# Gated infini-attention and SwiGLU on one core: six operands of x taken over from the first stage, eight made beside its last chains, fills of the stacks apart, and the feature map ahead of the remainder

## The chip, the cores and the metric

The kernel runs on one core of a Trainium2 chip. The metric is the device time of one execution in microseconds (us); the time before is the median of three runs. The engines are named as the profile names them: PE is the matrix engine, with PEld its weight loads, DVE the vector engine, ACT the scalar engine, POOL the engine called GpSimd, and SP the engine that issues the DMAs; SPq is its queue.

## The reference

The input `x` has 2048 rows of D = 576. A gate for each row mixes a memory-augmented attention with a feed-forward network.

```python
g = sigmoid((x * gate_w).sum(-1))              # one number per row
# a: H = 32 heads of 18, S = 2048 in 4 segments of L = 512
phi = where(t > 0, t + 1, exp(t))
for s in range(4):
    p = softmax(qs @ ks.T * 18 ** -0.5 + causal_mask)
    a_mem = (phi(qs) @ M) / (phi(qs) @ z + 1e-6)
    o = sigmoid(beta) * a_mem + (1 - sigmoid(beta)) * (p @ vs)
    M, z = M + phi(ks).T @ vs, z + phi(ks).sum()
a = concat(o) @ wo
# b: F = 4608
b = (silu(x @ w_gate) * (x @ w_up)) @ w_down
out = g * a + (1 - g) * b
```

## The kernel before

The products of the projections, of the network and of `wo` keep fp32 accuracy by splitting: `split(hi, lo, src)` (L103 to L105) writes a rounded copy of an operand on ACT (the high half) and the remainder on DVE (the low half), and PE multiplies high by high, high by low and low by high. A *chain* is one bank of PSUM filled by 14 such matmuls (`products`, L127). PSUM has eight banks; a small cycle of banks belongs to each kind of work, so a product waits until its bank has been read out.

**First stage (0 to about 231 us).** It works through the four segments of 512 rows.

- Nine `qk` chains of a segment make `q` and `k` transposed. Each result is split three ways into bf16 parts in `q3`: a copy on ACT (L314), the remainder `qr` on DVE (L315), its copy on ACT (L324), the last part on POOL (L325). SP stores `q3` to DRAM (`stk`), two chains later (`late`, `flush`). Chains whose feature map is wanted also make `ph`: Relu (L322) and Exp (L323) on ACT, then a combination on DVE (L327). In the list `mid` a caller may put work of its own between `qr` and Relu.
- Eight `v_step`s make `v` in banks 5, 6 and 7. Each has a plain copy `vf` (ACT, in segment 0 DVE, L345), a first bf16 part `vps` (ACT, L346), the remainder `r1` (DVE, L347), the second part (ACT) and the third (POOL), and in its second half a copy of the gate's logit, `gl` (DVE, L349). Beside them the next segment's x is split, one tile in a step.
- `upd_gen` updates the memory matrix during the next segment's chains: transposes, a copy `kt` on ACT (L378), the accumulating matmuls L369, then the masks (L389 to L393). `mem_step` reads the memory beside the `v_step`s (L415 to L422), and its result `om` goes to DRAM (`med`).

The x operands live in seven slots of two tiles, `xo00` to `xo61`, each with a high and a low half of 128 x 512. A segment's x fills slots 0 and 1 (segments 0 and 2) or 5 and 6 (segments 1 and 3); slots 2, 3 and 4 are staging for loads.

**Second stage.** The gate and up projections of the network use a scheme of seven block products (`seven`, L917) instead of eight: the operands of x are the blocks `c, d, e, g` of two segments and sums of them (`XO[0]` to `XO[6]`, two tiles `z` each; the sums are made in place on POOL by `x_sum`), and the weights likewise. One pass (`half`) covers segments 2 and 3, a second one segments 0 and 1. Each pass goes over 36 tiles `f` of 128 columns of F. A loop written out by hand runs the seven products of a tile, reads out the banks in between, and calls `tick` eight times; a tick runs `beat`, which first runs what `defer(k, fn)` has queued for that beat in `due`, then a share of the down projection (`down_group`, L765 and L770) and a step of the attention's generator (`att_gen`: scores L602 and L642, exp L646, the mask L654, casts L719 and L721, products with v L671 and L673). In the first pass `w_make(f)` makes the weight operands of the next tile: sums on POOL (`total`, L231), high halves on ACT (L235), low halves on DVE (L238), and SP keeps them in DRAM (`wc`, L248), from where the second pass fetches them.

**Between the stages.** After the last chains of segment 3, the memory of the q weights (pool `qp`) is closed and pools for the weights open in its place. `x_first()` loads eight x tiles of 256 KB into a pool `xrp` of its own, and returns a list of 14 steps: a split for each of the seven operands and two `z`, eight of them followed by a sum on POOL (L154 to L160). Two such steps are run in each of the `v_step`s 2 to 7 as far as four are left. The first weight operands (`start = w_make(0)`) begin in `v_step` 3, with up to 0, 3, 3, 6, 6 steps from there on; the rest of both lists is run ahead of the second stage. Then four stack tiles `kst` are filled with -1 by POOL (L587), the buffers `mb` with 0, and `stack_load(0)` issues the stack loads from `stk` on SP (L188), all in program order.

**Ahead of the end.** When the attention's generator is exhausted, `c_open` queues ten `wo_load`s. With n from 1 to 10, a load of 128 x 288 goes into one of three `woraw` buffers at beat n, the cast on ACT (L800) comes at beat n + 2, the low half on DVE (L801) at n + 3. The final loop then multiplies the attention by `wo`, mixes and stores.

Of the kernel before, what the change touches and what calls it, by code (L numbers as in the profile page):

```python
# [12 lines left out]
F32 = mybir.dt.float32  # L13
# [19 lines left out]
NT = 5  # L33
# [13 lines left out]
BREAK = 10  # L47
KR = 6 * DH
# [7 lines left out]
def gated_mix(ctx, tc, xT, wf, wd, wv, wo, beta, cmask, ident, bmask, out):  # L56
# [211 lines left out]
    with ExitStack() as st:  # L268
# [20 lines left out]
        def q_split(m, u):  # L289
            split(qw[m][0][:, u], qw[m][1][:, u], raws[m, u])  # L290
# [17 lines left out]
        def qk(s, m, u, mid=()):  # L308
            t = chain_tile()
            hi, lo = qw[m]  # L310
            products(t, w_stat(hi[:, u], lo[:, u]), x_side(*xs_of[s]))
# [3 lines left out]
            nc.vector.tensor_sub(qr, t, q3[:, 0])  # L315
            for fn in mid:
                fn()
            ph = None
            if m == 4 or (u == 0 and s > 0) or (u == 1 and s < 3):
                ph = sp.tile([P, L], F32, name=f"ph{m}{u}", bufs=2 if m == 4 else 1)  # L320
                phi[s, m, u] = ph
                nc.scalar.activation(ph, t, AF.Relu, scale=-1.0)  # L322
                nc.scalar.activation(ph, ph, AF.Exp, scale=-1.0)  # L323
            nc.scalar.activation(q3[:, 1], qr, AF.Copy)  # L324
            nc.gpsimd.tensor_sub(q3[:, 2], qr, q3[:, 1])  # L325
            if ph is not None:
                nc.vector.scalar_tensor_tensor(ph, t, 0.0, ph, op0=OP.max, op1=OP.add)  # L327
            if m < 4:
                late.append((stk[u, s, m * P:m * P + P], q3))
            else:  # L330
                for kind in range(2):
                    late.append((stk[kind, s, 512:D], q3[64 * kind:64 * kind + 64]))

        def v_step(s, hf, i):
# [7 lines left out]
            if s:  # L342
                nc.scalar.activation(fv, pv, AF.Copy)
            else:
                nc.vector.tensor_copy(fv, pv)  # L345
            nc.scalar.activation(v[:, i, :, 0, 0:DH], pv, AF.Copy)  # L346
            nc.vector.tensor_sub(r1, pv, v[:, i, :, 0, 0:DH])  # L347
            if hf:
                nc.vector.tensor_copy(gl[:, 4 * s + i:4 * s + i + 1], t[:, 288:289])  # L349
# [124 lines left out]
        def x_first():  # L474
            r = [[xrp.tile([P, L], F32, name=f"xr{b}{kt}") for kt in range(4)] for b in range(2)]
            for z in range(2):
                for b, kt in ((0, z), (1, z), (1, 2 + z), (0, 2 + z)):
                    nc.sync.dma_start(r[b][kt], xT[HALF[0][b], :, kt])
            X = [[None, None] for _ in range(7)]

            def four(z):
                return r[0][z], r[1][z], r[0][2 + z], r[1][2 + z]

            def one(j, z):
                c, d, e, g = four(z)
                X[j][z] = x_slot(j, z)
                split(X[j][z][:, 0], X[j][z][:, 1], (c, c, c, e, d, g, e)[j])
                for i, back in ((0, 1), (1, 2), (2, 4), (3, 6)):
                    if j == i:
                        x_sum(back, *four(z))  # L490

            return X, [lambda j=j, z=z: one(j, z) for j in range(7) for z in range(2)]

        for s in range(NSEG):
            upd = upd_gen(s - 1) if s else None
            casts = []
            for n, (m, u) in enumerate(chains):
# [13 lines left out]
                if (s, n) == (1, 7):  # L511
                    mid.append(betas)
                if s < 3:
# [6 lines left out]
            if s == 3:  # L520
# [30 lines left out]


    with ExitStack() as st:
        cps = []
        rw = pool(st, "rw", 4)
# [21 lines left out]
        while start[0][0] < 8:  # L577
            start.pop(0)[1]()
        while todo:
            todo.pop(0)()  # L580
        xst.close()
        kp = pool(ast, "kp", 2, side="right")
        ap = pool(ast, "ap", 2, side="right")
        for i in range(NST):
            qst.append(kp.tile([P, 2, L], BF, name=f"qst{i}", bufs=1))
            kst.append(kp.tile([P, 2, L], BF, name=f"kst{i}", bufs=1))
            nc.gpsimd.memset(kst[i], -1.0)  # L587
# [204 lines left out]
        def wo_load(n, hf, kt):  # L792
            box = []

            def load():
                box.append(cps[0].tile([P, 288], F32, name="woraw", bufs=3))
# [3 lines left out]
            defer(n + 2, lambda: nc.scalar.activation(wos[hf][:, 0, kt], box[0], AF.Copy))  # L800
            defer(n + 3, lambda: nc.vector.tensor_sub(wos[hf][:, 1, kt], box[0], f32(wos[hf][:, 0, kt])))  # L801
# [47 lines left out]
        due = deque()  # L849

        def defer(k, fn):
            while len(due) < k:
                due.append([])
            due[k - 1].append(fn)

# [23 lines left out]
        def x_second(new, xs):  # L879
# [10 lines left out]
            def parts(z, j):  # L890
                new[j][z] = x_slot(j, z)
# [214 lines left out]
```

## Time and profile before

| | |
|---|---|
| time, median of 3 runs | 1912.32 us (1911.87 to 1915.85) |
| the profiled execution: time | 1915.99 us |
| its span | 1914.2 us |
| its mean granted clock | 0.987 |
| PE / PEld busy | 1834.5 us (96%) / 1552.9 us (81%) |
| DVE / ACT / POOL busy | 1231.5 us (64%) / 965.6 us (50%) / 858.2 us (45%) |
| DMA | 330.83 MB, mean 173 GB/s; instruction fetches 0.5% of 16 engines |
| chain that ended last | PE 76%, ACT 6%, DVE 6%, DMA 5%, issue 4% |

| stretch, us | length | PE busy |
|---|---|---|
| 0 to 36 | 36 | 30.80 |
| 210 to 232 | 22 | 21.16 |
| 262 to 320 | 58 | 57.65 |
| 1400 to 1795 | 395 | 388.68 |
| 1825 to 1914.2 | 89.2 | 85.52 |

The span runs from the first to the last instruction that the profiler recorded; the time of the same execution lies 1.8 us above it. Busy shares are means over stages with different limits. In rows of the timeline, the columns are the start in us, the busy time of the group in us, engine, line, operation, output and inputs, the tile's shape, the number of instructions (x12), and in brackets the idle time of the engine ahead of it with what ended it. "<-DVE r L347" says that DVE's instruction of L347, which wrote r, was the last thing waited for. A line of the code that makes all products alike (L127, L917) stands for many tiles; the weights' names then tell which.

### The profile page before, as it was taken

How to read it: one execution, taken by the hardware profiler on the slowest of the kernel's cores; microseconds unless marked ns; L12 is line 12 of the kernel's file. 1: busy time of each engine (PE TensorE's matmuls, PEld its weight loads, DVE VectorE, ACT ScalarE, POOL GpSimd, SP SyncE). 2: the span in 40 equal slices, each digit the busy share in tenths (PEclk: the TensorE clock that was granted, in tenths of full speed). 3: DMA queues.
4: the chain of work that ended last, by engine and by line, in shares of the span. 5: the costliest groups of instructions: out<-in, count | busy, mean ns of one | idle time of the engine just before them, and what ended most of it. 6: DMA issues, size and time to landing. Idle time of an engine off the chain costs nothing.

```text
span 1914.2 us, 36563 instructions
## 1 busy us (share of the span) xinstructions
PE 1834.5 (96%) x12508; PEld 1552.9 (81%) x12508; DVE 1231.5 (64%) x3040; ACT 965.6 (50%) x1792; POOL 858.2 (45%) x1246
## 2 busy tenths in 40 slices
PE   8899889999999999999998999999999999999999
PEld 7798768778877887887787788788878878888899
DVE  5455666777777777777777665666565656655355
ACT  6566554566456556555644634444554454355211
POOL 3223632555545554554554544544445444444121
PEclk9999989999999999999999999999999999999999
DMA  6433475565475466456546635644554454445544
GB/s 224 138 131 141 165 251 197 187 218 184 135 237 184 155 206 228 161 167 222 189 147 227 213 112 156 197 142 124 177 177 137 128 189 140 141 155 155 180 152 141
DMA packets 204457, 330.83 MB, mean 173 GB/s; under 512 B 38192, under 2 KB 95664, under 8 KB 204272
## 3 DMA queue, kind: packets, MB, share of 16 engines
q1 hardware_dynamic: 204272, 328.50, 52.5%
q8 instruction: 100, 1.64, 0.4%
q14 instruction: 85, 0.70, 0.1%
HBM read 194.33 MB, written 134.09 MB: 172 GB/s over the span
## 4 chain that ended last, share of the span: by engine, by line
PE 76%; ACT 6%; DVE 6%; DMA 5%; issue 4%; POOL 2%; SPq 2%; ACTq 0%; DVEq 0%; POOLq 0%
PE bank L917 26%; PE bank L765 23%; PE bank L127 10%; PE bank L923 5%; PE bank L642 3%; PE bank L602 3%; PE bank L671 2%; PE bank L673 1%; ACT L646 1%; DMA draw<-in_wd_dram 1%; PE bank L369 1%; ACT pe L646 1%; ACT L991 1%; ACT hh L104 1%; PE bank L415 0%
## 5 line engine op out<-in xcount | busy, mean ns | idle before, releaser
L721 POOL TENSOR_TENSOR p<-pe,p 128x512 f16<-128x512 f32 x320 | 373.3, 1166 | 696.2 <-DVE p L719 616.5
L765 PE MATMUL bank<-dw,hh 128*128 128x288 f32 x2304 | 484.9, 303 | 17.4 <-DVE ya L770 13.1
L765 PEld LDWEIGHTS bank<-dw,hh 128*128 128x128 f32 x2304 | 380.8, 190 | 40.4 <-DVE ya L770 20.5
L646 ACT ACTIVATE pe<-bank 128x512 f32<-128x512 f32 x320 | 191.1, 597 | 337.5 <-PE bank L642 293.9
L765 PE MATMUL bank<-dw,hl 128*128 128x288 f32 x1152 | 341.7, 297 | 1.2 <-DVE hl L105 1.2
L770 DVE TENSOR_TENSOR ya<-bank,ya 128x288 f32<-128x288 f32 x352 | 160.0, 456 | 232.3 <-PE bank L765 230.2
L609 DVE CUSTOM_DVE_ANT_0 scr<-bank,cm 128x512 bf16<-128x512 f32 (+3 forms) x512 | 246.9, 482 | 15.1 <-PE bank L602 8.4
L765 PEld LDWEIGHTS bank<-dw,hl 128*128 128x128 f32 x1152 | 218.5, 190 | 1.7 <-DVE hl L105 1.7
L642 PE MATMUL bank<-qst,kst 111*128 111x512 bf16 (+3 forms) x512 | 151.9, 305 | 0.1
L719 DVE CAST p<-pe 128x512 f16<-128x512 f32 x320 | 150.9, 472 | 1.0 <-POOL pe L654 0.9
L654 POOL TENSOR_SCALAR_AFFINE_SELECT pe<-pe 128x256 f32<-128x256 f32 (+1 forms) x320 | 136.2, 426 | 13.5 <-ACT pe L646 12.1
L602 PE MATMUL bank<-kst,qst 108*128 108x512 bf16 (+3 forms) x512 | 126.6, 301 | 13.8 <-ACT pe L646 13.3
L998 DVE TENSOR_TENSOR bank<-bank,row 128x512 f32<-128x512 f32 x72 | 50.3, 698 | 105.7 <-ACT row L994 105.2
L985 ACT ACTIVATE row<-bank 128x512 f32<-128x512 f32 x72 | 43.1, 598 | 135.7 <-PE bank L923 135.3
L646 ACT ACT_TABLE_LOAD x66 | 84.7, 1283 | 46.3 <-PE bank L642 45.4
L105 DVE TENSOR_TENSOR hl<-row,hh 128x512 fp32r<-128x512 f32 x72 | 51.0, 708 | 84.4 <-ACT hh L104 84.4
L127 PE MATMUL bank<-xo,qhi 128*128 128x512 f32 x288 | 92.3, 401 | 5.2 <-ACT xo L104 5.1
L642 PEld LDWEIGHTS <-kst 111*128 111x128 bf16 x512 | 47.9, 97 | 53.8 <-issue 38.6
L325 POOL TENSOR_TENSOR q<-qr,q 128x512 bf16<-128x512 f32 x36 | 42.4, 1177 | 106.4 <-ACT q L324 102.9
L989 ACT ACTIVATE bank<-bank 128x512 f32<-128x512 f32 x72 | 41.9, 582 | 91.0 <-PE bank L917 86.1
L991 ACT ACT_TABLE_LOAD x67 | 86.0, 1283 | 1.2
L974 ACT ACTIVATE bank<-bank 128x512 f32<-128x512 f32 x72 | 42.0, 583 | 78.1 <-PE bank L917 68.4
(2084 smaller groups left out, 4280.1 us busy)
## 6 DMA issues: line engine op xcount, KB each, us to landing
raw<-in_wf_dram SPq DMA_DIRECT2D x72, 320.0 KB
dc<-dw SPq DMA_DIRECT2D x36, 576.0 KB
dw<-dc SPq DMA_DIRECT2D x36, 576.0 KB
stk<-q SPq DMA_DIRECT2D x32, 384.0 KB
draw<-in_wd_dram SPq DMA_DIRECT2D x36, 288.0 KB
vd<-vps SPq DMA_DIRECT2D x8, 912.0 KB
v<-vd SPq DMA_DIRECT2D x16, 456.0 KB
qst<-stk SPq DMA_DIRECT2D x128, 54.0 KB
```

The lines of the kernel that those rows point to most:

```text
L127: nc.tensor.matmul(t, st[n], mv[n], start=(n == 0), stop=(n == 13))
L602: nc.tensor.matmul(t[:, c:c + w], qs[:KR, pr, P * i:P * i + P], ks[:KR, pr, 0:w], start=True, stop=True)
L609: nc.vector.tensor_tensor_reduce(scr[:, :w], t[:, c:c + w], cm[:, L - w:L], 1.0, -3.0e38, OP.add, OP.max, m[:, k:k + 1])
L642: nc.tensor.matmul(t[:, c:c + w], ks[:KR + 3, pr, P * j:P * j + P], qs[:KR + 3, pr, P * j:L], start=True, stop=True)
L646: nc.scalar.activation(pe, t, AF.Exp, scale=SCALE)
L654: nc.gpsimd.affine_select(d, d, pattern=pat, compare_op=OP.is_ge, fill=0.0, base=0, channel_multiplier=-1)
L719: nc.vector.tensor_copy(p1, pe)
L721: nc.gpsimd.tensor_sub(p2, pe, p1)
L765: nc.tensor.matmul(t, p, q[:, cs], start=(n == 0), stop=(n == 3 * CH - 1))
L770: nc.vector.tensor_add(ya[:, i, cs], t, ya[:, i, cs])
L917: nc.tensor.matmul(t, w[:, p, z], x[z][:, q], start=first and n == 0, stop=last and n == 5, skip_group_check=True)
L991: nc.scalar.activation(sg0, sg0, AF.Silu)
```

## The change

Four things are changed together.

- **Operands of x for the first pass.** `SLOT` maps operands to slots, so that operands 0, 3 and 5 (six tiles) are the tiles that segments 2 and 3 have already split for their own products. The other eight tiles are made for the pass: their x tiles are loaded in chains 2 to 5 of segment 3 into memory that is no longer used (`first_load`: the q weights of finished chains, now one tile for each `u`, and two `ph` tiles). Operands 1, 4 and 2 are summed on POOL in chains 4, 5 and 7 and split in chains 6, 7 and 8; operand 6 is summed in `v_step`s 0 and 1 and split after the last one. `x_first`, its pool, eight of its loads after the chains and six of its 14 splits are gone. The second pass uses the same map.
- **Weights of the first tile.** `w_make(0)` starts ahead of the `v_step`s, with up to 2 or 3 of its steps in each from the third on.
- **Fills.** The first `kst` tile is filled where it was; the other three are deferred to beats 1, 3 and 5. `due` and `defer` are defined earlier for that.
- **Order in the first stage, and `wo`.** In `qk`, Relu and Exp follow the first copy directly, with `qr` and `mid` behind them. In `v_step`, the `vf` copy of segment 0 comes behind `r1`. `woraw` has four buffers, and each cast and low half comes one beat later.

```diff
+SLOT = (0, 3, 2, 1, 4, 6, 5)
...
-            sh = [P, 2 if m < 4 else 1, NT, P]
-            qw.append((qp.tile(sh, F32R, name=f"qhi{m}"), qp.tile(sh, F32R, name=f"qlo{m}")))
+            qw.append([[qp.tile([P, NT, P], F32R, name=f"{z}{m}{u}") for u in range(2 if m < 4 else 1)] for z in ("qhi", "qlo")])
...
             nc.scalar.activation(q3[:, 0], t, AF.Copy)
-            nc.vector.tensor_sub(qr, t, q3[:, 0])
-            for fn in mid:
-                fn()
             ph = None
             if m == 4 or (u == 0 and s > 0) or (u == 1 and s < 3):
...
                 nc.scalar.activation(ph, t, AF.Relu, scale=-1.0)
                 nc.scalar.activation(ph, ph, AF.Exp, scale=-1.0)
+            nc.vector.tensor_sub(qr, t, q3[:, 0])
+            for fn in mid:
+                fn()
             nc.scalar.activation(q3[:, 1], qr, AF.Copy)
...
             if s:
                 nc.scalar.activation(fv, pv, AF.Copy)
-            else:
-                nc.vector.tensor_copy(fv, pv)
             nc.scalar.activation(v[:, i, :, 0, 0:DH], pv, AF.Copy)
             nc.vector.tensor_sub(r1, pv, v[:, i, :, 0, 0:DH])
+            if not s:
+                nc.vector.tensor_copy(fv, pv)
...
-        def x_first():
...
+        def first_load(n):
+            for q, (b, kt) in enumerate((((0, 0), (1, 0)), ((1, 2), (0, 1)), ((1, 1), (1, 3)), ((0, 2), (0, 3)))[n]):
+                if n < 3:
+                    r = qp.tile([P, NT * P], F32, name=f"{('qhi', 'qlo')[q]}{n}0")[:, :L]
+                else:
+                    r = sp.tile([P, L], F32, name=f"ph{q}1", bufs=1)
+                rx[b, kt] = r
+                nc.sync.dma_start(r, xT[HALF[0][b], :, kt])
+
+        def first_sum(j, z):
+            c, d, e, g = (rx.get(k) for k in ((0, z), (1, z), (0, 2 + z), (1, 2 + z)))
+            o, p, q = {1: (c, d, c), 4: (d, g, d), 2: (g, g, c), 6: (e, e, g)}[j]
+            nc.gpsimd.tensor_sub(o, p, q)
+
+        def first_split(j, z):
+            XO[j][z] = x_slot(SLOT[j], z)
+            split(XO[j][z][:, 0], XO[j][z][:, 1], rx[{1: (0, z), 4: (1, z), 2: (1, 2 + z), 6: (0, 2 + z)}[j]])
+
+        FSUM = {4: [(1, 0), (4, 0)], 5: [(2, 0), (1, 1)], 7: [(4, 1), (2, 1)]}
+        FSPLIT = {6: [(1, 0), (4, 0)], 7: [(2, 0), (1, 1)], 8: [(4, 1), (2, 1)]}
...
+                if s == 3:
+                    if 2 <= n < 6:
+                        first_load(n - 2)
+                    for j, z in FSUM.get(n, []):
+                        mid.append(lambda j=j, z=z: first_sum(j, z))
+                    for j, z in FSPLIT.get(n, []):
+                        mid.append(lambda j=j, z=z: first_split(j, z))
...
-                xst = ExitStack()
-                xrp = pool(xst, "xrp", 1, side="right")
-                XO, todo = x_first()
+                for z in range(2):
+                    for j, b, kt in ((0, 2, z), (3, 2, 2 + z), (5, 3, 2 + z)):
+                        XO[j][z] = xs_of[b][0][kt]
                 wraw_of[0] = [w_load(0, u) for u in range(2)]
+                start = w_make(0)
...
-                    for _ in range(2 if n > 1 else 0):
-                        if len(todo) > 4:
-                            todo.pop(0)()
-                    if n == 3:
-                        start = w_make(0)
-                    for _ in range((0, 0, 0, 0, 3, 3, 6, 6)[n]):
+                    if n < 2:
+                        first_sum(6, n)
+                    for _ in range((0, 0, 2, 3, 3, 3, 3, 3)[n]):
                         if start[0][0] < 8:
                             start.pop(0)[1]()
         flush()
+        while start[0][0] < 8:
+            start.pop(0)[1]()
+        for z in range(2):
+            first_split(6, z)
...
-        while start[0][0] < 8:
-            start.pop(0)[1]()
-        while todo:
-            todo.pop(0)()
-        xst.close()
...
-            nc.gpsimd.memset(kst[i], -1.0)
+            if i:
+                defer(2 * i - 1, lambda i=i: nc.gpsimd.memset(kst[i], -1.0))
+            else:
+                nc.gpsimd.memset(kst[i], -1.0)
...
-                box.append(cps[0].tile([P, 288], F32, name="woraw", bufs=3))
+                box.append(cps[0].tile([P, 288], F32, name="woraw", bufs=4))
...
-            defer(n + 2, lambda: nc.scalar.activation(wos[hf][:, 0, kt], box[0], AF.Copy))
-            defer(n + 3, lambda: nc.vector.tensor_sub(wos[hf][:, 1, kt], box[0], f32(wos[hf][:, 0, kt])))
+            defer(n + 3, lambda: nc.scalar.activation(wos[hf][:, 0, kt], box[0], AF.Copy))
+            defer(n + 4, lambda: nc.vector.tensor_sub(wos[hf][:, 1, kt], box[0], f32(wos[hf][:, 0, kt])))
...
-                new[j][z] = x_slot(j, z)
+                new[j][z] = x_slot(SLOT[j], z)
```

More of the change, by code (lines that the diff above doesn't have):

```diff
@@ L289, in q_split @@
         def q_split(m, u):
-            split(qw[m][0][:, u], qw[m][1][:, u], raws[m, u])
+            split(qw[m][0][u], qw[m][1][u], raws[m, u])
         def v_load(hf, a, b):
@@ L310, in qk @@
             hi, lo = qw[m]
-            products(t, w_stat(hi[:, u], lo[:, u]), x_side(*xs_of[s]))
+            products(t, w_stat(hi[u], lo[u]), x_side(*xs_of[s]))
             q3 = sp.tile([P, 3, L], BF, name="q3", bufs=4)
@@ L472, in gated_mix @@
         halves = {3: VW[0], 6: VW[1], 7: VW[2], 8: VW[3]}
-        def x_first():
[L475 to L492, printed above, removed]
+        XO = [[None, None] for _ in range(7)]
+        rx = {}
+        def first_load(n):
[15 more added lines that the diff above has]
+        FSPLIT = {6: [(1, 0), (4, 0)], 7: [(2, 0), (1, 1)], 8: [(4, 1), (2, 1)]}
         for s in range(NSEG):
@@ L550, in gated_mix, with defer @@
         flush()
+        while start[0][0] < 8:
+            start.pop(0)[1]()
+        for z in range(2):
+            first_split(6, z)
     with ExitStack() as st:
         cps = []
+        due = deque()
+        def defer(k, fn):
+            while len(due) < k:
+                due.append([])
+            due[k - 1].append(fn)
         rw = pool(st, "rw", 4)
@@ L847, in gated_mix @@
         yas = {}
[L849 to L854, printed above, removed]
         def split_by(k, hi, lo, src):
```

## Prediction

> **What bounds the kernel now.** I read the busy shares first, then the busy time by stretch, then PE's timeline in every stretch where PE is not full, and there the engine that it waits for.
>
> ```profile
> PE 1834.5 (96%) x12508; PEld 1552.9 (81%) x12508; DVE 1231.5 (64%) x3040; ACT 965.6 (50%) x1792; POOL 858.2 (45%) x1246
> 36.00:72.00 36.00, 30.59 (x180) 27.28 (x179) 19.23 (x42) 20.51 (x42) 11.70 (x14) 0.95 0.41 140
> 72.00:210.00 138.00, 137.37 (x817) 122.93 (x816) 68.83 (x185) 78.84 (x158) 43.20 (x52) 1.00 0.35 128
> 232.00:262.00 30.00, 17.81 (x58) 12.86 (x59) 18.47 (x40) 14.74 (x35) 15.21 (x19) 0.77 0.49 173
> 1795.00:1825.00 30.00, 26.88 (x110) 20.94 (x109) 13.71 (x25) 13.96 (x30) 5.44 (x6) 0.89 0.85 280
> ```
>
> Columns of the stretches: length, busy PE, PEld, DVE, ACT, POOL, granted clock, DMA share, GB/s. PE sets the end, so only its idle or slow time can be won. It is full from 72 to 210 us. Three stretches have room: 36 to 72 (5.4 us idle), 232 to 262 (12.2 us idle, clock 0.77) and 1795 to 1825 (3.1 us idle, clock 0.89). The two programs' instruction orders differ only in front of 262 us and in the ten loads, casts and remainders of `wo` behind 1795; the 1,533 us between are the same instructions in the same order.
>
> ```profile
> 48.88 1.85 PE L127 MATMUL bank<-vw,xo 128*128 128x290 f32 x12 [1.11 <-DVE r L347]
> 52.16 1.85 PE L127 MATMUL bank<-vw,xo 128*128 128x290 f32 x12 [1.17 <-DVE gl L349]
> 67.69 2.73 PE L369 MATMUL bank<-vf,kt 128*128 128x152 f32 x10 [2.89 <-ACT kt L378]
> 44.51 0.43 ACT L346 ACTIVATE vps<-bank 128x288 bf16<-128x288 f32 x1 [1.25 <-DVE vf L345]
> ...
> 62.35 0.60 ACT L322 ACTIVATE ph<-bank 128x512 f32<-128x512 f32 x1 [1.31 <-DVE qr L315]
> ```
>
> In front, PE waits for PSUM banks that DVE frees late; DVE and ACT hand work to and fro, and ACT waits for DVE's `vf` copy and for `qr`.
>
> ```profile
> 243.82 2.93 PE L917 MATMUL bank<-xo,wo__2429 128*128 128x512 f32 x6 [2.57 <-ACT bank L974]
> ...
> 261.04 1.41 PE L917 MATMUL bank<-xo,wo__2614 128*128 128x512 f32 x4 [4.50 <-DVE row L1002]
> 245.71 3.63 POOL L587 MEMSET kst<- 128x1024 bf16 x4 [4.59 <-DVE wo__2474 L238]
> 242.65 0.32 SPq L306 DMA_DIRECT2D med<-om  x1
> 246.68 0.72 SPq L188 DMA_DIRECT2D kst<-stk  x1
> 254.11 0.34 SPq L248 DMA_DIRECT2D wc<-wo__2470  x1
> 259.42 0.42 ACT wo__2630 L235
> ```
>
> Between the stages the last hole (4.50 us) is decided far from PE: the first fill of `kst` (245.71), twelve stack loads on SP, `v` and `draw`, only then the store of `wo__2470` (254.11, 5.23 us until its buffer is free), the cast, two DVE steps, PE at 261.04. From fill to PE that is 15.33 us.
>
> ```profile
> 1804.23 0.44 ACT L800 ACTIVATE wo<-woraw 128x288 fp32r<-128x288 f32 x1 [2.18 <-DMA woraw<-in_wo_dram]
> 1806.47 1.66 PE L917 MATMUL bank<-xo,wo__23838 128*128 128x512 f32 x6 [1.78 <-DVE bank L998]
> 1809.16 2.90 PE L917 MATMUL bank<-xo,wo__23855 128*128 128x512 f32 x6 [1.03 <-issue]
> ```
>
> **Front (v steps of segment 0, feature map first).** A step's loop before is vf 0.45 (DVE), vps 0.43 (ACT), r 0.46 (DVE), second part 0.46 (ACT), high half of x 0.61 (ACT), low half 0.81 (DVE): 3.24 us, as the r's at 45.04, 48.27 and 51.49 repeat. With vf behind r, vf runs on DVE under ACT's work, and the next vps runs under DVE's low half: r + 0.46 + 0.61 + 0.81 = 2.34, minus the overlap of two ACT instructions, about 2.25. PE's step is 1.87, but three banks stand between. Stepping it through: banks come free at 44.2, 46.4 and 48.75, PE asks at 45.3, 47.1 and 49.0. So its waits of 0.19, 1.11 and 1.17 go, and segment 1 starts at 50.9 instead of 54.1. There Relu and Exp no longer wait 0.8 to 1.3 us for `qr`; `qr` itself comes 0.6 later, under Exp. The chain to the first `kt` then ends at about 60.5, PE asks at 61.2, so the 2.89 goes too. The ten L369 that followed the hole took 2.53 us to the next instruction (67.69 to 70.22) against 1.21 in the next round. Their end moves from 70.22 to 62.4: 7.8. The margins are 0.2 to 0.7 us, so I take **7.5**, with 5.0 (the kt wait stays) and 7.8 as ends.
>
> [...]
>
> **Chains of segment 3.** Eight x loads of 256 KB now sit on SP between stores of `stk`, each behind a chain or a transpose that is done (the latest at about 195); six sums (1.17 alone, 1.35 to 1.48 beside DVE) go to POOL, which is busy 43 of 138 us there; six highs (0.61, ACT) and six lows (0.70 alone, 1.2 beside a POOL sum, DVE) go into the last three chains. PE needs none of it at once: after the ninth chain come `v_step`s in other banks. DVE's backlog: lows 4 x 1.2 + 2 x 0.7, less the idle 1.9 + 1.3 that L392 and L315 had there, leaves r of the first v step at 214.8 instead of 212.4. Its bank is asked for at 217.2, and the `om` that frees bank 3 ends at 216.4 against 216.6. Cost 0, and 1.3 if a low takes 0.2 longer each; the cover is thin.
>
> **Between the stages.** Gone from the v steps: 12 of the 14 highs and lows (13.0 us of DVE in all) and six of eight sums (8.5 us of POOL). Added: a new wait. The first weight load is issued only once the last x sum has left the memory of `qp`: POOL's order puts it behind two v remainders at 219.7, against 213.45 before. Behind it on SP wait two `stk` stores, `med`, `vd` and the next weight load; the first user, an `om` buffer at 226.6, still has 1 us. But 2 MB of x no longer stand ahead: the load then took 5.98; the kernel's first load of this kind took 2.91, and two in a row make some 3.5, so the weights land at 223.5, and the first weight sum starts there instead of at 230.94. Six weight steps now sit between v steps; the last v step's `om` ends at about 235.3 (242.6 before), its store `med` is issued at 235.5 and lands within 3.05 (242.65 to 245.71): the `kst` fill starts at 238.6. Plus the unchanged 15.33, PE goes on at 253.9: **7.1** won. PE itself starts stage two at 230.7, waits 2.0 for the `xx` copy (ACT has two highs of x ahead of it, 235.5), and reaches the same instruction at about 246. So a hole of some 7.5 us stays; the bound is SP, not x. After the hole of 4.50 the next 18 L917 took 5.76 instead of 4.08, 1.7 lost; a longer hole may cost up to 1.3 more, I take 0.6. Net **6.5**; ends 3.5 (weights need the full 5.98) and 9.5 (`med` lands in 1.5 and the wc store in 4).
>
> The four fills apart give nothing here: SP waits for the first alone, the other three ran beside its issues. Put into POOL's queue at ticks 1, 3 and 5 (0.95 each) they delay weight sums by 1.9 us; those then end near 243, needed at 253: 0. Taking over six operands and the new slot order change no instruction of the second half but addresses: 0.
>
> **Tail.** Four `woraw` buffers and casts one tick later give a load about 1.5 us more (a tick without down groups, PE 1794.26 to 1801.5 for five). ACT waited 10.2 us in eight casts. The first two casts fall behind L989 and L994, so L998 moves from 1805.7 to about 1802.8, and the 1.78 and 1.03 go; but loads take 4 to 5.5 us at a DMA share of 1.0, and L974 of the next f still waits for the third and fourth (1808.7 instead of 1810.35). PE's third product there moves from 1811.86 to about 1809.3. **2.5**; ends 0 (bandwidth decides) and 5 (the slow clock, 2.90 and 2.76 for what takes 1.36, goes as well).
>
> **Sum.** 7.5 + 6.5 + 2.5 = 16.5. The profiled execution has a span of 1914.2 and a time of 1915.99, 3.7 above the median of the runs shown (1912.32); the holes do not explain that difference, so I take the sum from the median: **1895.8 us** (span 1897.7).
>
> **Rivals.**
> First: the front wait is only moved. If PE asks for kt 1 us too early or the banks' 0.25 margin is missed, only the start of segment 1 moves (3.2): 1900.1. For it: thin margins; against it: two waits on that chain go at once. Chance 0.15.
> Second: the new weight wait decides. If the weights land 3 us later, ACT's casts stand in its queue, the last `om` and with it the fill slip by as much, and perhaps the tail gives nothing: 1898.8 to 1901.3. For it: the 5.98 of before; against it: those were behind x. Chance 0.15.
> Third, slower: the stores of `wc`. ACT's casts wait for the buffer six operands back, as at 259.42. If the backlog of DMA at the restart (share 1.0 from 256.5 to 270) lasted, because PE now arrives with SP further behind, each f could lose the 4.5 us of that hole. It decides from four such repeats on (18 us); with five the time is 1918. PE's idle time from 262 to 1795 was 48.6 us; it would pass 66. Against it: same order, and the restart is set by the same chain. Chance 0.05.
> Fourth: what is freed in front and between is waited for at the fill again, because the fill hangs on something that does not move: 1912. No wait shows that. Chance 0.03.
>
> **How the numbers follow.** The forecast has 0.62. Its own ends are 1912.3 - 22.3 = 1890 and 1912.3 - 8.5 = 1903.8; the first two rivals lie inside. I give 1889 to 1904. A measurement of this kernel can tell about 0.2% (3.8 us) from no change: faster 0.92, same 0.03, slower 0.05.
>
> **What would show it.** Right: PE without a wait over 0.3 us between 44 and 70 and segment 1 starting near 50.9; no x sums behind 220 (less the 7.5 won); the first `kst` fill some 14.6 earlier than 245.7, PE's one large hole then 6 to 9 us and ended by the same L1002; casts L800 behind L994. Wrong: a PE wait on L378 that stays, a first weight sum behind 226 (less 7.5), or idle time of the second stage above 55 us.

## The result, and the profile after

The changed kernel takes 1900.19 us, the median of five runs (1898.39 to 1905.98); beside it the kernel before took 1914.22 (1911.87 to 1917.30, five runs). The ratio is 0.9935, with a 95% interval of 0.9912 to 0.9958: about 12.4 us less by the ratio, 14.0 by the medians. A second set on one chip gave 1899.79 against 1913.01, ratio 0.9933 (0.9921 to 0.9945). The forecast was 1895.8, with 1889 to 1904 as its range. The profiled execution took 1899.41 us at a span of 1897.6.

The page's busy line:

```profile
PE 1822.3 (96%) x12508; PEld 1546.4 (81%) x12508; DVE 1222.2 (64%) x3034; ACT 961.5 (51%) x1786; POOL 856.1 (45%) x1246
```

The busy time by stretch, in the columns used before. The stretches are those shown of before, moved to where the same work now lies:

```profile
36.00:64.50 28.50, 28.50 (x182) 26.45 (x181) 19.26 (x42) 19.84 (x42) 10.92 (x12) 1.00 0.54 186
64.50:202.50 138.00, 138.00 (x827) 124.46 (x826) 71.29 (x192) 83.25 (x165) 51.39 (x58) 1.00 0.41 144
224.50:254.50 30.00, 20.35 (x74) 14.98 (x73) 14.46 (x37) 13.33 (x30) 10.07 (x14) 0.83 0.72 253
1778.00:1808.00 30.00, 25.35 (x115) 20.20 (x114) 13.90 (x25) 14.65 (x30) 5.84 (x6) 1.00 0.92 314
```

The front is full, where 5.4 us were idle. Between the stages 9.7 of 30 us are still idle (12.2 before). Ahead of the end 4.7 of 30 are idle (3.1 before), but at a clock of 1.00 instead of 0.89.

PE's timeline after, first the group that followed the kt wait, then the waits that are left:

```profile
61.82 1.38 PE L369 MATMUL bank<-vf,kt 128*128 128x152 f32 x10
...
208.65 0.90 PE L415 MATMUL bank<-Mm,ph 128*128 128x152 f32 x6 [0.75 <-DVE om L422]
220.41 0.90 PE L415 MATMUL bank<-Mm,ph 128*128 128x152 f32 x6 [1.13 <-DVE om L422]
247.27 2.90 PE L927 MATMUL bank<-xo,wo__2600 128*128 128x512 f32 x6 [6.72 <-DVE row L1012]
1791.98 1.62 PE L927 MATMUL bank<-xo,wo__23841 128*128 128x512 f32 x6 [1.44 <-DMA wo__23841<-wc]
1794.70 1.66 PE L927 MATMUL bank<-xo,wo__23853 128*128 128x512 f32 x6 [1.10 <-ACT bank L984]
1806.66 0.53 PE L782 MATMUL bank<-dw,hh 128*128 128x288 f32 x2 [1.68 <-ACT hh L105]
```

The group of L369 comes without a wait and takes 1.38 us instead of 2.73. Two short waits stand at L415 in segment 3's v steps, where the kernel before had one of 0.67 us. The hole between the stages is longer (6.72 against 4.50), but it ends 13.8 us earlier. In the tail two waits of 1.44 and 1.10 us stand in the place of 1.78 and 1.03, and a new one at hh follows.

What leads to the hole, on POOL, ACT and SP (SPq is SP's queue of issues):

```profile
216.08 0.73 POOL L232 TENSOR_TENSOR ws<-raw 128x256 f32<-128x256 f32 x1 [3.50 <-DMA raw<-in_wf_dram]
231.50 0.95 POOL L604 MEMSET kst<- 128x1024 bf16 x1 [5.28 <-DMA med<-om]
239.75 0.41 SPq L249 DMA_DIRECT2D wc<-wo__2428  x1
245.64 0.42 ACT L236 ACTIVATE wo__2616<-ws 128x256 fp32r<-128x256 f32 x1 [7.55 <-DMA wc<-wo__2428]
```

The first weight sum comes 14.9 us earlier than before and the first fill 14.2. Behind the fill the chain of before repeats: SP's stack loads, then the store of `wo__2428`, then the cast that waits for its buffer.

**Where the time came from.** PE runs the same 12,508 matmuls in the same order in all kernels here, so the same instruction can be set against itself. The table shows how many us each kernel gained on the profiled execution of before between one landmark of PE and the next; each number is the difference of two starts in the timelines. The landmarks, by their start before and in the changed kernel: 9.86 (10.52), 70.22 (63.03, the L377 behind the first group of L369), 209.55 (200.74, the first v step of segment 3), 230.42 (223.12, the last L415), 265.69 (252.97, an L917 behind the hole), 1794.26 (1779.04) and the end.

| kernel | to 9.9 | to 70.2 | to 209.6 | to 230.4 | to 265.7 | to 1794 | to the end |
|---|---|---|---|---|---|---|---|
| changed | -0.7 | 7.8 | 1.6 | -1.5 | 5.4 | 2.5 | 1.4 |
| changed, again | -0.8 | 7.4 | 1.6 | -1.8 | 5.1 | 4.6 | 0.5 |
| front_only | -0.5 | 7.4 | 1.6 | 0.0 | -1.1 | 4.7 | 0.2 |
| relu_only | -0.9 | 2.4 | 1.6 | 0.0 | -1.4 | 6.9 | -0.7 |
| vf_only | 0.2 | 7.2 | 0.2 | 0.0 | -0.6 | 5.6 | -0.6 |
| xops_only | -0.1 | 0.1 | -0.1 | -2.0 | 5.1 | 1.8 | -0.1 |
| tail_only | -0.3 | 0.0 | -0.1 | 0.0 | -0.2 | 4.7 | 0.9 |

The sixth column is a stretch in which none of these kernels changes an instruction, and yet all are 1.8 to 6.9 us ahead in it: there the profiled execution of before lost more than any of the others (the last section has the clock's part). So 2.5 of the 16.6 us between the two profiled executions are not put down to the change. Without them 14.1 are left, which fits the 14.0 of the medians; the second profiled execution of the changed kernel gives 12.1 in the same way, which is nearer to the 12.4 of the ratio.

### The profile page after: what moved, and what is told of

Its sections match the earlier page's. It is cut to its first block, busy times and chain, and to the rows that moved or that the text cites. A ratio compares the mean times of both kernels' runs of the same rounds, so it can differ in the third digit from the quotient of the medians.

```text
span 1897.6 us, 36543 instructions
## 1 busy us (share of the span) xinstructions
PE 1822.3 (96%) x12508; PEld 1546.4 (81%) x12508; DVE 1222.2 (64%) x3034; ACT 961.5 (51%) x1786; POOL 856.1 (45%) x1246
## 3 DMA queue, kind: packets, MB, share of 16 engines
q8 instruction: 100, 1.64, 0.4%
## 4 chain that ended last, share of the span: by engine, by line
PE 77%; DVE 6%; DMA 6%; ACT 5%; issue 4%; SPq 2%; POOL 1%; DVEq 0%; ACTq 0%; POOLq 0%
PE bank L927 26%; PE bank L782 23%; PE bank L128 11%; PE bank L933 5%; PE bank L619 3%; PE bank L659 3%; PE bank L688 2%; PE bank L690 1%; ACT L663 1%; PE bank L369 1%; DMA draw<-in_wd_dram 1%; ACT pe L663 1%; ACT L1001 1%; PE bank L415 1%; SPq L189 1%
## 5 line engine op out<-in xcount | busy, mean ns | idle before, releaser
L984 ACT ACTIVATE bank<-bank 128x512 f32<-128x512 f32 x72 | 42.0, 583 | 78.4 <-PE bank L927 68.4
```

## The experiments

Each kernel was timed beside the kernel before on the same chip, in three sets; the medians of the kernel before were 1913.01, 1913.43 and 1913.58 us. Differences from the kernel before are worked out from the ratio.

**The three parts alone, and the whole again.** front_only is the kernel before with these edits:

```diff
 # qk: Relu and Exp of ph moved ahead of these
+            nc.vector.tensor_sub(qr, t, q3[:, 0])
+            for fn in mid:
+                fn()
 # v_step
-            else:
-                nc.vector.tensor_copy(fv, pv)
...
             nc.vector.tensor_sub(r1, pv, v[:, i, :, 0, 0:DH])
+            if not s:
+                nc.vector.tensor_copy(fv, pv)
```

> The kernel before with the order of the first stage alone: Relu and Exp ahead of qr, and the vf copy of segment 0 behind r1. Theory (two waits on one chain go at once): PE without a wait over 0.3 us between 44 and 70, the kt wait of 2.89 gone, and about 7.5 us less than before in the front; with the bank wait in segment 2's v steps that this order also removed in the changed kernel (1.2), 7 to 9 us less in all. Rival (the wait is only moved to the kt copy): 3 us less. Rival (the gain of the front is waited for again at the fill of kst): no change.

Measured: 1903.78 us (1898.85 to 1904.86), ratio 0.9949 (0.9938 to 0.9961), 9.8 less (7.5 to 11.9; expected 7 to 9). PE has no wait from 36 to 72 us. 7.4 us come from the front and 1.6 from segment 2; neither rival holds, since the lead of 8.5 us is still there when stage two begins.

xops_only is the changed kernel with the order of the first stage, the fills and the woraw lines of before:

```diff
-            if i:
-                defer(2 * i - 1, lambda i=i: nc.gpsimd.memset(kst[i], -1.0))
-            else:
-                nc.gpsimd.memset(kst[i], -1.0)
+            nc.gpsimd.memset(kst[i], -1.0)
...
-                box.append(cps[0].tile([P, 288], F32, name="woraw", bufs=4))
+                box.append(cps[0].tile([P, 288], F32, name="woraw", bufs=3))
```

> The kernel before with the operands of x alone: six taken over, eight made beside the last chains, the first tile's weights started earlier; the four fills of kst together, woraw with three buffers and the old order of the first stage. Theory: the first weight sum some 15 us earlier than 230.9, the first kst fill some 15 us earlier than 245.7, a larger hole of PE ahead of the same restart (6 to 8 us against 4.50), bank and om waits of 1 to 2 us in segment 3's v steps, net 4 to 6 us less than before. Rival (the new wait of the first weight load decides): less than 3 us. Rival (stores of wc fall behind for good): slower, and PE's idle time in the second stage over 60 us.

Measured: 1907.34 us (1903.68 to 1912.65), ratio 0.9976 (0.9966 to 0.9985), 4.6 less. By the table it loses 2.0 us in segment 3's v steps and wins 5.1 behind them. The "15 us earlier" of the expectation was a slip: it counted the front's lead, which this kernel doesn't have. The first weight sum moved from 230.94 to 225.38, the first fill from 245.71 to 241.92, 3.8 us, where the prediction's step said 7.1. PE's hole ahead of the restart was 5.76 us, just under the 6 to 8 expected. PE's idle time behind the hole was 49.4 us of 1532, against 48.65 of 1533 before, so stores did not fall behind for good.

tail_only is the kernel before with the last edit:

```diff
-                box.append(cps[0].tile([P, 288], F32, name="woraw", bufs=3))
+                box.append(cps[0].tile([P, 288], F32, name="woraw", bufs=4))
...
-            defer(n + 2, lambda: nc.scalar.activation(wos[hf][:, 0, kt], box[0], AF.Copy))
-            defer(n + 3, lambda: nc.vector.tensor_sub(wos[hf][:, 1, kt], box[0], f32(wos[hf][:, 0, kt])))
+            defer(n + 3, lambda: nc.scalar.activation(wos[hf][:, 0, kt], box[0], AF.Copy))
+            defer(n + 4, lambda: nc.vector.tensor_sub(wos[hf][:, 1, kt], box[0], f32(wos[hf][:, 0, kt])))
```

> The kernel before with four woraw buffers and the casts of wo one beat later, nothing else. Theory: 1.5 to 2.5 us less, the casts of wo behind the read-outs of L989 and L994, the waits ahead of L917 of the last tile 1 to 2.5 us in all. Rival (the bandwidth of DMA decides there, share 0.85 to 0.92): no change, the same holes ended by DMA.

Measured: 1910.92 us (1907.27 to 1913.95), ratio 0.9992 (0.9984 to 1.0001), 1.5 less, with no change inside the interval. The two waits ahead of L917 are 1.74 and 1.08 us, no shorter than the 1.78 and 1.03 before and a little over the 2.5 expected. The table's 0.9 is what is left of 2.7 us: PE is that far ahead when the tile ends, and then waits 1.42 us at hh.

> The changed kernel once more, beside its parts. Theory (three terms that add up): 14 to 17 us less than before, and within 2 us of the sum of front_only, xops_only and tail_only. Rival (the parts stand in one chain and share a gain): the parts add up to over 3 us more than the whole.

Measured: 12.8 us less by the ratio (10.5 to 15.1). The parts add up to 9.8 + 4.6 + 1.5 = 15.9, 3.1 more than the whole: past the 2 of the theory and the 3 of the rival, but inside the intervals of the four. The traces point the other way: up to 230.4 the columns of the parts add up to the whole's within 0.5 us, from there to 265.7 the parts give -1.1 + 5.1 - 0.2 = 3.8 and the whole 5.1 to 5.4. So a gain that the parts share is not shown; two us either way are within what single executions scatter.

**Which half of the front.** relu_only is front_only without the v_step edit, vf_only front_only without the qk edit.

> The kernel before with Relu and Exp ahead of qr, and the vf copy where it was. Theory (the bank waits of 1.11 and 1.17 in segment 0's v steps hang on the vf copy, the kt wait of 2.89 and the slow group of L369 on the feature map alone, and each keeps its gain): the two bank waits stay, the kt wait goes, and with segment 2's bank wait of 0.6 the front gains 5 to 6 us. Rival (the kt wait goes only if both parts act): the kt wait shrinks by 1 us or less, and the gain is under 2.5 us.

> The kernel before with the vf copy of segment 0 behind r1, and Relu and Exp where they were. Theory: the two bank waits go, segment 1 starts about 3 us earlier and the kt wait of 2.89 stays or grows, since the chain to kt hangs on qr as before; in all 3 us less, and segment 2's bank wait of 0.62 stays. Rival (PE asks for kt earlier by the same 3 us and the chain to kt does not move): the kt wait grows by the 3 us and there is no change.

Measured: relu_only 1909.05 us (1906.33 to 1915.86), ratio 0.9984 (0.9971 to 0.9996); vf_only 1904.35 us (1903.17 to 1907.88), ratio 0.9964 (0.9950 to 0.9977). PE at the kt wait, relu_only and then vf_only:

```profile
67.41 1.48 PE L369 MATMUL bank<-vf,kt 128*128 128x152 f32 x10 [1.12 <-ACT kt L378]
```

```profile
61.54 1.48 PE L369 MATMUL bank<-vf,kt 128*128 128x152 f32 x10 [0.49 <-ACT kt L378]
```

What ACT did before and then in vf_only, at the start of segment 1's first chain:

```profile
60.47 0.58 ACT L314 ACTIVATE q<-bank 128x512 bf16<-128x512 f32 x1
```

```profile
54.42 0.58 ACT L314 ACTIVATE q<-bank 128x512 bf16<-128x512 f32 x1
```

Both theories fell, and so did vf_only's rival of no change. Feature map first did not remove the kt wait, it shortened it from 2.89 to 1.12 (the bank waits of 1.11 and 1.16 stayed, as expected); and the vf copy behind r1, which was to leave that wait alone, shortened it to 0.49. The trace says why: ACT and DVE reach segment 1's first chain only when the last v step's work is done, and the first copy of that chain (L314) starts at 60.47 before and at 54.42 in vf_only, 6.05 us earlier, while PE reaches the segment only 3.4 us earlier. Each half takes most of the wait, so their gains (7.2 and 2.4) don't add up to the 7.4 of both. The edit that seemed to be about banks gave nearly all of the front; the other one is worth 1.6 us in segment 2, where it let DVE begin the v steps earlier.

**Fills together.** The changed kernel with the four fills in one row again (the first edit of xops_only).

> The changed kernel with the four fills of kst together again. Theory (SP waits for the first fill alone): within 0.2% of the changed kernel, the first fill and the restart of PE where they were. Rival (SP's first stack load or the weight sums wait for all four fills): PE restarts 2.8 us later, the time 2 to 3 us above 1900.

Measured: 1899.35 us (1893.97 to 1902.63), ratio 0.9922 (0.9907 to 0.9937). The first fill is at 231.02, PE goes on at 245.68. The fills apart bring nothing, as predicted.

**Segment 3 and the hole.** sum6_early runs the two sums of operand 6 before the pool of the q weights is closed:

```diff
             if s == 3:
+                for z in range(2):
+                    first_sum(6, z)
                 qst_.close()
...
-                    if n < 2:
-                        first_sum(6, n)
```

> The changed kernel with the two sums of operand 6 made on POOL ahead of the v steps instead of in them. Theory (the first weight load waits for the last x sum, and SP's queue with it; the store of om behind it then holds PE at L415): the first weight load is issued 2 to 3 us earlier than 211.91, the wait of 1.13 us of L415 on om at 220.4 is gone, the other one (0.75 at 208.65, DVE behind four lows of x) stays, and 1 to 2 us less than the changed kernel. Rival (the om wait is DVE's backlog as well): both waits stay and there is no change.

Measured: 1898.11 us (1895.90 to 1899.22), ratio 0.9920 (0.9908 to 0.9932). The first weight load goes at 208.80 instead of 211.91, the wait at 220.4 is gone, the other one stays (1.01): the theory. The first fill also came earlier, 228.68 instead of 231.50, and PE's restart with it. Against the changed kernel's ten runs (1897.67 to 1905.98, median 1899.99) the 1.9 us are in the expected size, but the ranges overlap.

keeps_first runs more of the first tile's steps ahead of the stack loads, so that four stores (`wo__2428`, `wo__2467`, `wr__2469`, `wo__2475`) are issued before them:

```diff
         flush()
-        while start[0][0] < 8:
+        while start[0][0] < 9:
             start.pop(0)[1]()
+        for i in (0, 0, 1, 2):
+            start.pop(i)[1]()
```

> The changed kernel with four more stores of the first tile's weight operands (wo__2428, wo__2467, wr__2469, wo__2542) issued on SP ahead of the stack loads. Theory (the hole of 6.72 us ahead of L1012 is set by SP: twelve stack loads, v and draw stand ahead of the store that the cast waits for): the cast of wo__2616 comes at about 239 instead of 245.64, the hole shrinks to under 3 us, and 3 to 5 us less than the changed kernel's 1900. Rival (x or the weights' own path sets the restart, SP is only late beside it): the same hole, ended by another wait, and no change against 1900. Rival (the transfers share one bandwidth): the stack loads land later by as much, the next hole opens at the scores L619, and no change.

Measured: 1898.31 us (1895.20 to 1900.15), ratio 0.9919 (0.9907 to 0.9932). ACT's casts, then PE:

```profile
238.00 0.41 ACT L236 ACTIVATE wo__2616<-ws 128x256 fp32r<-128x256 f32 x1
...
246.32 0.42 ACT L236 ACTIVATE wo__2664<-ws 128x256 fp32r<-128x256 f32 x1 [5.16 <-DMA wc<-wo__2556]
```

```profile
250.81 2.93 PE L929 MATMUL bank<-xo,wo__2642 128*128 128x512 f32 x6 [5.48 <-DVE bank L993]
```

The cast of `wo__2616` moved to 238.00 as the theory said, but the hole did not shrink below 3 us. It moved on to `wo__2642`: the cast of `wo__2664` waits for the next store, which still stands behind the stack loads (issued at 240.13). The theory named the right queue and one store too few. The median is 1.7 us under that of the changed kernel's ten runs, where 3 to 5 were expected, and the ranges overlap.

sums_keeps has the same stores and spreads the x work over earlier chains:

```diff
-        FSUM = {4: [(1, 0), (4, 0)], 5: [(2, 0), (1, 1)], 7: [(4, 1), (2, 1)]}
-        FSPLIT = {6: [(1, 0), (4, 0)], 7: [(2, 0), (1, 1)], 8: [(4, 1), (2, 1)]}
+        FSUM = {4: [(1, 0), (4, 0)], 5: [(2, 0), (1, 1)], 6: [(4, 1), (2, 1)], 8: [(6, 0), (6, 1)]}
+        FSPLIT = {5: [(1, 0), (4, 0)], 6: [(2, 0), (1, 1)], 7: [(4, 1), (2, 1)]}
...
-                    if n < 2:
-                        first_sum(6, n)
```

> The changed kernel with the stores of keeps_first, the sums of operands 4 and 2 for z = 1 one chain earlier, those of operand 6 in the last chain, and the splits one chain earlier each. Theory (three separate waits: 0.75 at the bank, 1.13 at om, 6.72 behind SP): both waits in segment 3's v steps gone, the first weight load near 206 instead of 211.91, the hole under 3 us, and 5 to 8 us less than the changed kernel, 1892 to 1895. Rival (the fill of kst sets the restart and does not move with the weights): no better than keeps_first. Rival (more work in the last chains pushes PE at L415 back): the waits in the v steps grow past 2 us and eat half of it.

Measured: 1892.04 us (1890.35 to 1893.14), ratio 0.9887 (0.9872 to 0.9901), all four runs under all ten of the changed kernel. Both waits in the v steps are gone, the first weight load is issued at 204.96, the first fill starts at 227.20: the rival that the fill does not move with the weights is out. The hole is as in keeps_first, 5.80 us at `wo__2642`, where under 3 was expected. So the expected time (1892 to 1895) came without the closing of the hole. Against the changed kernel, PE is 2.4 us better at the last L415 by the table's measure, and the fill is 4.3 us earlier, where keeps_first had left it at 231.49.

stack_late lets that next store pass as well:

```diff
-        for pr in range(2):
-            stack_load(0, pr)
+        stack_load(0, 0)
+        defer(6, lambda: stack_load(0, 1))
...
-        v_fetch(0)
+        defer(8, lambda: v_fetch(0))
```

> sums_keeps with the second pair's stack loads behind the sixth beat's work and the first load of v behind the eighth's, so that the store of the seventh operand goes ahead of four stack loads. Theory (the hole of 5.80 us that is left ahead of wo__2642 is still SP's order, one store further on: the cast of wo__2664 waited 6.03 us for a store issued at 236.07): that store goes at about 232, the hole shrinks to 1 to 3 us, and 2 to 4 us less than sums_keeps' 1892. Rival (the stack loads of the second pair or the next store are then late): a hole of the same size at L619 or one operand later, and no change.

Measured: 1889.11 us (1887.75 to 1889.51), ratio 0.9878 (0.9861 to 0.9896), all runs under those of sums_keeps. PE:

```profile
242.71 1.65 PE L927 MATMUL bank<-xo,wo__2642 128*128 128x512 f32 x6 [0.73 <-DVE bank L991]
...
249.75 1.67 PE L927 MATMUL bank<-xo,wo__2722 128*128 128x512 f32 x6 [1.06 <-DVE bank L1008]
253.84 1.66 PE L927 MATMUL bank<-xo,wo__2749 128*128 128x512 f32 x6 [1.03 <-ACT bank L984]
```

The hole is 0.73 us, and three waits of about 1 us or less come behind it. So the hole left in sums_keeps was the order of SP's issues, and nothing had to be made faster to close it. 5.07 us of hole were worth 2.9 us between the medians, since part comes back in the waits behind it.

casts_later adds one more beat and one more buffer in the tail:

```diff
-                box.append(cps[0].tile([P, 288], F32, name="woraw", bufs=4))
+                box.append(cps[0].tile([P, 288], F32, name="woraw", bufs=5))
...
-            defer(n + 3, lambda: nc.scalar.activation(wos[hf][:, 0, kt], box[0], AF.Copy))
-            defer(n + 4, lambda: nc.vector.tensor_sub(wos[hf][:, 1, kt], box[0], f32(wos[hf][:, 0, kt])))
+            defer(n + 4, lambda: nc.scalar.activation(wos[hf][:, 0, kt], box[0], AF.Copy))
+            defer(n + 5, lambda: nc.vector.tensor_sub(wos[hf][:, 1, kt], box[0], f32(wos[hf][:, 0, kt])))
```

> stack_late with five woraw buffers and the casts of wo one more beat later. Theory (the tail's gain is given back because late loads of wo still hold ACT ahead of the read-outs: waits of 2.72, 0.97, 1.10 and 1.36 us in L817, then 1.10 at L927 and 1.68 at hh): those two waits of PE shrink to under 1 us together, 1 to 2 us less than stack_late. Rival (bandwidth: at a DMA share of 0.92 loads land later, not earlier, the more are under way): the 1.44 of PE behind the operand from wc grows by what the others lose, and no change.

Measured: 1887.53 us (1886.51 to 1889.15), ratio 0.9869 (0.9849 to 0.9890). PE's wait behind ACT's L984 is gone, the wait at hh is 0.45 instead of 1.28, the one for the operand from `wc` 1.55 instead of 1.49. The 1.6 us between the medians fit the theory, but the ranges of the two kernels meet. It is the fastest kernel of these, 25.1 us under the kernel before by the ratio (21.0 to 28.9).

## Why the prediction was right, and where it was not

**Front: right, and for a step that was named in passing.** Predicted 7.5 with ends of 5.0 and 7.8; the table has 7.2 to 7.8. The loop of 2.25 us per step is there: ACT's second parts (L350) in vf_only start at 47.98, 50.19 and 52.52. PE's margins held. The prediction put the kt wait's end down to the feature map's order as much as to the vf copy; the runs showed that the vf copy alone nearly does it. As for the clock, the profile's row at the slow group gave 0.50 from 67.2 to 70.6 us, behind a wait of 2.89; in the changed kernel it is 1.00 from 36.0 to 64.5 us, and the group takes 1.38 us instead of 2.73. (The six terms of the old loop add up to 3.22, not 3.24; nothing hangs on it.)

**Left out: segment 2.** The new order in `qk` also takes a bank wait of 0.62 us at L415 out of segment 2's v steps. In PE's timeline of before:

```profile
159.59 0.90 PE L415 MATMUL bank<-Mm,ph 128*128 128x152 f32 x6 [0.62 <-DVE om L422]
```

PE gains 0.9 us at this instruction, and the rest of the 1.6 to the next landmark in steps of 0.1 to 0.3 around the L369 groups, which no wait shows. The prediction looked at the feature map only where kt waited, although the 138 us from 72 on were 0.63 short of full.

**Chains of segment 3: the term that was mis-sized.** "Cost 0, and 1.3 if a low takes 0.2 longer each". The lows took longer by more than that. DVE's timeline after, a low half of x alone and two beside sums on POOL:

```profile
196.55 0.68 DVE L106 TENSOR_TENSOR xo<-qlo,xo 128x512 fp32r<-128x512 f32 x1
...
200.46 1.78 DVE L106 TENSOR_TENSOR xo<-qhi,xo 128x512 fp32r<-128x512 f32 x1
202.16 1.76 DVE L106 TENSOR_TENSOR xo<-qlo,xo 128x512 fp32r<-128x512 f32 x1
```

POOL's sums beside them, and then the same two lows in sums_keeps:

```profile
200.40 1.29 POOL L489 TENSOR_TENSOR qhi<-qlo,qhi 128x512 f32<-128x512 f32 x1
201.77 1.61 POOL L489 TENSOR_TENSOR qlo<-qlo,qlo 128x512 f32<-128x512 f32 x1
```

```profile
200.13 0.68 DVE L106 TENSOR_TENSOR xo<-qhi,xo 128x512 fp32r<-128x512 f32 x1
200.73 0.68 DVE L106 TENSOR_TENSOR xo<-qlo,xo 128x512 fp32r<-128x512 f32 x1
```

1.78 and 1.76 against the 1.2 of the prediction; the two lows of the last chain took 1.05 and 1.65. Together that is 6.24 us where the prediction had 4.8, DVE begins the v steps late (r at 215.8 in the prediction's clock, where it had 214.8), and PE waits 0.75 us. In sums_keeps, where the sums stand elsewhere, these two lows take 0.68 each and that wait is gone. Each of the four slow lows ends 0.54 to 0.56 us behind the end of an instruction on POOL; what holds them there, these runs do not show. The second wait, 1.13, was the one looked for at om ("still has 1 us"): the weight load's wait on SP held the store of om, and sum6_early took it away.

**Between the stages: right in kind, 2.6 us too much.** Predicted 6.5 net; the columns to 230.4 and to 265.7 give -1.5 + 5.4 = 3.9. In the prediction's clock (the 8.81 us of lead at the first v step of segment 3 added) the fill came at 231.50 + 8.81 = 240.3 instead of 238.6, and PE went on at 256.1 instead of 253.9. In xops_only the first weight load was issued at 220.92 instead of 219.7, and its first sum started at 225.38 instead of 223.5. In the changed kernel `med` took 3.75 us from its issue at 227.75 to the fill, instead of 3.05. From fill to PE it was 15.77 instead of 15.33. (The "twelve stack loads" of the prediction are ten; twelve issues it is with `v` and `draw`.) "The bound is SP, not x" held, as stack_late shows. The large hole was there as forecast, 6.72 against 7.5, ended by the same line.

**Tail: half of it, and not by the waits.** Predicted 2.5; 0.5 to 1.4 measured. The wait of 1.78 went as told, but the one of 1.03 came back as 1.44, now for an operand from `wc`, and one of 1.10 behind ACT's L984 is new: 2.81 us became 2.54. By the end of the tile PE was 3.2 us further ahead all the same, most of it because the slow clock was gone (2.90 and 2.76 became 1.62 and 1.66), which the prediction had kept for its end of 5. That was not the edit's doing alone: in relu_only, vf_only and xops_only, which have the tail of before, these two groups take 1.62 to 1.66 as well, and yet their last column is -0.7 to -0.1. What PE wins there it waits for again. The step that was missing is this end of the tile: its last products go by faster, their read-outs on ACT stand behind the casts of late loads, and PE meets hh too early (1.68). The end "bandwidth decides" is not it, or not alone: with later casts most of the wait at hh went (1.28 to 0.45 us in casts_later), while the one for the operand from `wc` stayed (1.49 to 1.55).

**The sum.** The front came out as 7.8 for 7.5, the chains and what lies between the stages together as 3.9 for 6.5, the tail as 1.4 for 2.5; segment 2 gave 1.6 that was not in the sum, and 0.7 were lost ahead of 9.9 us, where nothing of the change lies and the runs scatter by as much. The 16.5 us came out as 14.1, or 12.4 by the ratio. That the forecast came within 4.4 us owes something to luck: the 1.6 of segment 2 stood in for part of what the other terms missed. That the sum was made from the median and not from the profiled execution was right: that execution lost more in the long stretch that no kernel here changed, as the sixth column shows.

**The rivals.** "Front only moved" is out (front_only). "The weight load's new wait decides" is in part what happened, with about 2 us of its 3. "Stores of wc for good" is out: PE's idle time in the long stretch was 50.1 us of 1530.5, not over 66. "Nothing gained" is out.

## What to carry to other kernels

When a wait is taken out, follow the helper engines' queue, not only the wait that PE shows: two edits can take the same wait away, and a whole chain behind them moves by the larger one. A hole that a DMA's landing ends may be set by that DMA's place in the issuing queue; the order of issues was worth as much here (1.7 and 2.9 us between medians in keeps_first and stack_late) as the work saved (4.6 in xops_only), and the next store in the queue is the next bound. Where an unchanged stretch differs between two profiled executions, take it out of the comparison first; with the same instruction order on PE, each instruction can be set against itself.

## What the runs showed of the hardware

The clock went to half speed behind an idle time of PE of 2.07 us in one execution, and stayed at full speed behind one of 2.06 in another. The same wait of PE in the long stretch, before and then in the changed kernel, in PE's timeline:

```profile
486.17 0.38 PE L602 MATMUL bank<-kst,qst 108*128 108x128 bf16 x2 [2.07 <-ACT pe L646]
```

```profile
473.08 0.38 PE L619 MATMUL bank<-kst,qst 108*128 108x128 bf16 x2 [2.06 <-ACT pe L663]
```

Twin waits, and only the first was followed by half clock. These are stretches of 3.41 us around the two waits (columns as above, the clock behind POOL), in the kernel before and then in the changed one:

```profile
483.63:487.04 3.41, 1.34 (x8) 0.89 (x7) 2.76 (x8) 3.38 (x8) 1.59 (x2) 1.00 0.68 201
487.04:490.45 3.41, 3.41 (x13) 3.05 (x13) 2.76 (x8) 1.08 (x3) 2.91 (x4) 0.50 0.54 176
```

```profile
468.02:471.44 3.42, 2.47 (x11) 1.38 (x11) 2.74 (x7) 1.73 (x4) 0.00 (x0) 1.00 0.90 298
471.44:474.85 3.41, 1.77 (x10) 1.51 (x10) 3.34 (x11) 3.40 (x7) 2.10 (x3) 1.00 0.52 174
474.85:478.26 3.41, 3.41 (x24) 3.21 (x24) 3.26 (x8) 0.17 (x1) 3.06 (x4) 1.00 0.46 163
```

Before, the stretch with the wait has 2.07 us of idling, and the next 3.41 us ran at 0.50. In the changed kernel the two stretches that the wait touches have 0.95 and 1.64 us of idling, and they and the next one ran at 1.00. From the instruction behind the wait to the first L917 behind the down group it took 5.55 us before (486.17 to 491.72) and 3.98 in the changed kernel (473.08 to 477.06): 1.57 us were lost. What decides whether the clock goes to half behind such a wait, these runs do not show.

Such stretches probably account for a good part of the sixth column, and so for part of the difference between runs of one kernel. In that column's stretch the kernel before has seven stretches of 3.41 us at 0.50, the changed kernel five. At 1.57 us each, two fewer would be 3.1 us, and the column has 2.5. Over the whole span the mean granted clock was 0.987 before, 0.993 in both executions of the changed kernel, 0.992 in relu_only, vf_only and xops_only, and 0.989 in front_only and tail_only; these last two are 4.7 ahead in the column all the same, so the clock is not all of it.
